# A code-dense step moved behind four products, and two filler matmuls near the start

## The chip, the cores and the metric

The kernel runs on one core of a Trainium2 chip. The metric is the device time in microseconds (us); lower is better. Engines are named as the profile names them: PE multiplies matrices (PEld is its weight load, which runs beside it), DVE, ACT and POOL are the vector, scalar and general engines, and SP issues the DMAs.

## The reference

Two layers follow each other. For each of 8 batches and 8 heads, 576 positions are gathered into 32 memory slots and read back; the result goes through a gated layer with a causal convolution of five taps:

```python
a = softmax(phi)                             # over the 576 positions, for each slot
k_m, v_m = a^T k, a^T v                      # 32 x 64 for each head
attn = softmax(scale * q k_m^T)              # over the 32 slots
x = attn v_m                                 # 576 x 512 for each batch
gate = sigmoid(sum_k conv_w[k] * shift(x, k))
out = (gate * (x @ w_val)) @ w_out
```

## The kernel before

Each matrix step works on one batch b. The products by `w_val` and the gates are made in halves of 288 positions (s), the last product in chunks of 128 output rows (c, 36 in all). The steps that matter here, by name:

- `phi_turn`, `phi_exp`: the softmax weights of the slots. `slots.b` sums keys and values into them (L467): four heads x five chunks x two groups, 40 small matmuls of 32 columns of weights. Batch 0 does this apart for keys (`slots.0.0.1`, `slots.0.1.1`: group 0 and 1) and values (`slots.0.0.0`, `slots.0.1.0`).
- `slots_inv`, `slots_scale`, `slots_turn`, `slots_place` (L474 to L498, L264): divide by the sums (DVE, then ACT or DVE), transpose on PE, and copy to `kvT`.
- `scores.b.s` (L514) multiplies by q; `scores_turn`, `soft_top`, `soft_exp`, `soft_norm`, `soft_turn` are the second softmax on DVE, POOL and ACT. `soft_turn.b.s` writes the rows pT that the following steps read.
- `conv.b.s` (L626, 40 matmuls) makes the gate's input with the taps already in the weights; from batch 2 on `mix.b.s` (L626, 8 matmuls) makes x, and `tap`, `scaled` and `add` apply the taps on DVE, ACT and POOL.
- `value.b.s.t` (L692): six matmuls of 288 columns for one of four column blocks t. Two blocks share two banks of PSUM, which `gated.b.s.y` (L698, DVE) reads together with the gate and gives back. `gated_high` and `gated_low` (L264, L267) split the result into two parts, which `project.c.y` (L727) multiplies by `w_out`.
- `spread_taps` (L388) repeats the convolution's weights; `warm.n` (L280) is a matmul of n x 128 columns of the identity that nobody reads.

All steps stand in one table, `ORDER`, written out by hand. Each engine executes its instructions in the order in which the table issues them; a star swaps the engine of a step. Nothing else orders them but semaphores between writers and readers.

PSUM has 8 banks of 512 floats. `take` gives a step the banks that have been free longest by the order of the table, and `drop` returns them. So a step that is added or moved in the table also changes which banks later steps get, and whose release they wait for.

In the profile, one float32 matmul of the program stands as two instructions of PE and two of PEld; the 40 matmuls of a slots step are x80 there. The split matmuls of L692 and L727 stand as one each.

Of the kernel before, what the change touches and what calls it, by code (L numbers as in the profile page):

```python
# [53 lines left out]
ORDER = """  # L54
warm.4 warm.4 load_top.0.0 load_w.c.0 load_top.0.1 phi_max.0.0 narrow_size.c.0 phi_open.0.0 phi_max.0.1 phi_open.0.1
narrow_round.c.0 phi_turn.0.0 warm.2 narrow_sign.c.0 load_kv.0.0.1 phi_turn.0.1 warm.2 phi_place.0.1 phi_place.0.0*
load_kv.0.1.1 slots.0.0.1 load_w.v.1 narrow_size.v.1 slots.0.1.1 narrow_add.c.0 load_q.0.0 slots_inv.0.1
narrow_round.v.1 spread_taps.1 slots_scale.0.1 place_taps.1 load_w.o.0 load_top.1 slots_turn.0.1 narrow_sign.v.1
narrow_round.o.0 narrow_size.o.0 slots_place.0.1* load_q.0.1 load_kv.0.0.0 scores.0.0 narrow_add.v.1 scores_turn.0.0
soft_top.0.0 phi_max.1 warm.4 soft_exp.0.0 load_kv.0.1.0 phi_open.1.0 warm.4 spread_taps.0 scores.0.1 place_taps.0  # L60
# [20 lines left out]
place.2 add.1.0.1.4 store.0 slots_place.2 phi_shift.3 scores.2.0 load_kv.3.0 tap.1.0.1.3 place.3 scaled.1.0.2.1  # L81
load_rest.3 scaled.1.0.3.1 scores.2.1 value.1.0.0 scaled.1.0.3.2 scores_turn.2.0 add.1.0.1.2 add.1.0.1.1 load_kv.3.1
load_top.4 scores_turn.2.1 value.1.0.1 soft_top.2* open_gate.1.0.0 gated.1.0.0 phi_exp.3 soft_exp.2 add.1.0.1.3
conv.1.1 slots.3 gate.1.1.1 gated_high.1.0.0 soft_norm.2 value.1.1.2 gate.1.1.0 phi_max.4 slots_inv.3 open_gate.1.0.1
value.1.1.3 gated.1.1.1 soft_turn.2.0 slots_scale.3* value.1.0.2 load_q.3 value.1.0.3 gated.1.0.1 gated_low.1.0.0
value.1.1.0 mix.2.0 gated_high.1.1.1 scaled.2.0.2.1 scaled.2.0.2.4 scaled.2.0.3.0 gated_low.1.1.1* value.1.1.1
scaled.2.0.2.0 tap.2.0.1.0 scaled.2.0.3.1 gated_high.1.0.1* slots_turn.3 project.5.0 gated.1.1.0 load_rest.5
project.4.0 soft_turn.2.1 tap.2.0.1.3 tap.2.0.0.0 store.3 scaled.2.0.2.3 slots_place.3* tap.2.0.0.4 gated_low.1.0.1
tap.2.0.1.1 scaled.2.0.3.3 gated_high.1.1.0 scaled.2.0.3.4 load_rest.4 project.4.1 load_top.5 tap.2.0.0.2 load_kv.4.0
# [735 lines left out]
```

## Time and profile before

| | us |
|---|---|
| three runs | 236.61, 237.48, 239.53 (median 237.48) |
| the profiled execution | 237.75 |
| its span, first to last instruction | 236.0 |
| PE busy | 226.2 (96%) |
| DVE / ACT / POOL busy | 185.4 / 169.4 / 170.2 |

The profile describes the execution of 237.75 us; 1.75 us of it lie outside the span. Start times count from the start of the span. A matmul's end is modelled, so a stretch is best measured from the start of its first matmul to the start of the next step's first.

### The profile page before, as it was taken

What the parts mean: (1) busy time and instruction counts of PE and PEld (TensorE: products, weight loads), DVE (VectorE), ACT (ScalarE), POOL (GpSimd) and SP (SyncE); (2) the same over time, 40 slices, a digit from 0 to 9 for tenths busy, and PEclk for the clock granted to TensorE, in tenths of its full rate; (3) what the DMA queues carried; (4) which work ended last, traced back from release to release, by engine and by line L of the source; (5) the groups of instructions that cost most, each with busy time, mean ns of one, the idle gap of its engine ahead of it and who ended that gap; (6) DMA issues with size and microseconds to landing.
All of it is one profiled execution on the core that took longest, in us unless ns stands there. A gap on an engine that the chain in (4) does not pass through costs nothing.

```text
span 236.0 us, 6170 instructions
## 1 busy us (share of the span) xinstructions
PE 226.2 (96%) x2496; PEld 175.1 (74%) x2496; DVE 185.4 (79%) x304; ACT 169.4 (72%) x338; POOL 170.2 (72%) x132
## 2 busy tenths in 40 slices
PE   7788999999989999999999999999999999999994
PEld 2536688777677589677887869787886687888882
DVE  2258828998868999978989879998999979759330
ACT  3369999659738797988878877498898654894302
POOL 1244879979866987999887979589958785955600
PEclk9979999999999999999999999999999999999998
DMA  6999999959958985376741999603801211121114
GB/s 190 372 413 404 416 410 385 416 207 335 364 138 287 420 287 219 99 274 227 247 157 37 327 375 350 259 0 111 267 7 44 87 49 46 44 92 44 44 64 159
DMA packets 14653, 51.17 MB, mean 217 GB/s; under 512 B 1658, under 2 KB 1954, under 8 KB 11938
## 3 DMA queue, kind: packets, MB, share of 16 engines
q1 hardware_dynamic: 14626, 50.79, 58.5%
q8 instruction: 19, 0.31, 0.6%
q14 instruction: 8, 0.07, 0.1%
HBM read 41.35 MB, written 9.44 MB: 215 GB/s over the span
## 4 chain that ended last, share of the span: by engine, by line
PE 90%; DMA 4%; ACT 2%; SPq 1%; issue 1%; POOL 1%
PE banks L727 43%; PE banks L692 22%; PE banks L467 8%; PE banks L626 6%; PE banks L514 4%; DMA q<-in_first_dram 4%; PE banks L593 3%; PE banks L280 1%; PE banks L436 1%; PE banks L498 1%; POOL w_val_sb L381 1%; PE banks L388 1%; ACT o L367 0%; SPq L308 0%; SPq L341 0%
## 5 line engine op out<-in xcount | busy, mean ns | idle before, releaser
L670 POOL TENSOR_TENSOR gate<-gate,x 128x576 f32<-128x576 f32 x49 | 71.7, 1464 | 15.4 <-ACT gate L662 5.3
L727 PE MATMUL banks<-woH,hL 128*128 128x512 f32 x144 | 58.2, 404 | 0.0
L727 PE MATMUL banks<-woH,hH 128*128 128x512 f32 x144 | 56.4, 392 | 0.0
L727 PE MATMUL banks<-woL,hH 128*128 128x512 f32 x144 | 56.3, 391 | 0.0
L662 ACT ACTIVATE x<-banks,cwP 128x288 f32<-128x288 f32 x104 | 48.6, 529 | 5.7 <-PE banks L626 3.7
L653 DVE SCALAR_TENSOR_TENSOR gate<-banks,cwP,gate 128x288 f32<-128x288 f32 x104 | 49.1, 508 | 2.1 <-ACT gate L651 1.2
L267 POOL TENSOR_TENSOR hL<-h,hH 128x576 fp32r<-128x576 f32 (+8 forms) x38 | 38.0, 1019 | 7.8 <-DVE hH L264 4.5
L698 DVE SCALAR_TENSOR_TENSOR h<-gate,banks 128x576 f32<-128x576 f32 x32 | 23.9, 749 | 16.5 <-PE banks L692 12.5
L727 PEld LDWEIGHTS banks<-woH,hL 128*128 128x128 f32 x144 | 27.0, 188 | 9.3 <-issue 2.1
L727 PEld LDWEIGHTS banks<-woH,hH 128*128 128x128 f32 x144 | 27.0, 188 | 6.0
L741 ACT ACTIVATE o<-banks 128x512 f32<-128x512 f32 x26 | 15.7, 603 | 21.1 <-PE banks L727 19.6
L727 PEld LDWEIGHTS banks<-woL,hH 128*128 128x128 f32 x144 | 27.1, 188 | 4.6
L692 PE MATMUL banks<-pL,vwH 128*128 128x288 f32 x128 | 28.6, 305 | 0.0
L692 PE MATMUL banks<-pH,vwH 128*128 128x288 f32 x128 | 27.3, 294 | 0.0
L692 PE MATMUL banks<-pH,vwL 128*128 128x288 f32 x128 | 27.3, 294 | 0.0
L692 PEld LDWEIGHTS banks<-pL,vwH 128*128 128x128 f32 x128 | 21.2, 188 | 6.1 <-issue 3.6
L264 ACT CAST hH<-h 128x576 fp32r<-128x576 f32 (+8 forms) x38 | 18.8, 531 | 7.3 <-DVE h L698 7.3
L267 POOL TENSOR_TENSOR pL<-pT,pH 128x1152 fp32r<-128x1152 f32 (+1 forms) x8 | 19.0, 2372 | 6.4 <-DVE pH L264 6.4
L467 PE MATMUL banks<-kv,e 128*32 128x129 f32 (+2 forms) x656 | 19.3, 263 | 2.8 <-issue 1.4
L675 ACT ACTIVATE gate<-gate 128x576 f32<-128x576 f32 x26 | 18.1, 699 | 4.0 <-DVE gate L653 2.8
L467 PEld LDWEIGHTS banks<-kv,e 128*32 128x32 f32 x656 | 16.3, 128 | 5.7 <-issue 5.3
L692 PEld LDWEIGHTS banks<-pH,vwL 128*128 128x128 f32 x128 | 20.5, 188 | 0.0
(96 smaller groups left out, 369.5 us busy)
## 6 DMA issues: line engine op xcount, KB each, us to landing
kv<-in_kv_dram SPq DMA_DIRECT2D x14, 1032.0 KB, 8.2
out_dram<-o SPq DMA_DIRECT2D x35, 256.0 KB, 2.6
q<-in_q_dram SPq DMA_DIRECT2D x7, 1152.0 KB, 8.4
phT<-in_phi_t_dram SPq DMA_DIRECT2D x7, 576.0 KB, 6.8
e<-in_phi_dram SPq DMA_DIRECT2D x6, 640.0 KB, 7.0
raw<-in_w_val_dram SPq DMA_DIRECT2D x4, 512.0 KB, 10.9
q<-in_first_dram SPq DMA_DIRECT2D x2, 576.0 KB, 9.7
rest<-in_kv_rest_dram SPq DMA_DIRECT2D x4, 258.0 KB, 2.9
```

Of the source, the lines that this page charges most:

```text
L264: eng.copy(out=out, in_=x) if eng is nc.scalar else eng.tensor_copy(out=out, in_=x)
L267: eng.tensor_tensor(out=out, in0=x, in1=hi.bitcast(F32), op=ALU.subtract)
L467: nc.tensor.matmul(km[j * M:(j + 1) * M, i, n], lhsT=e[:, i, j * M:(j + 1) * M, c], rhs=kvx[c][:, j, :], start=(c == 0), stop=(c == C - 1))
L626: nc.tensor.matmul(live["cv", b, s, g][x * D:(x + 1) * D, t, 0:n], lhsT=weights(g)[rows], rhs=pTs[b % 2][rows, g, s * HALF + i:s * HALF + ...
L653: nc.vector.scalar_tensor_tensor(out=gt, in0=v, scalar=w, in1=gt, op0=ALU.mult, op1=ALU.add)
L662: nc.scalar.activation(out=live[n][:, x], in_=live["cv", b, s, g][:, x, i:i + HALF], func=AF.Identity, scale=cwP[:, 0, i * NP + t:i * NP + ...
L670: eng.tensor_tensor(out=gt, in0=gt, in1=live["x", b, s, g, i], op=ALU.add)
L675: nc.scalar.activation(out=gt, in_=gt, func=AF.Tanh, scale=0.5)
L692: nc.tensor.matmul(vp[:, x, 0:HALF], lhsT=a[:, g, t * P:(t + 1) * P], rhs=p[:, g, s * HALF:(s + 1) * HALF], start=(i == 0), stop=(i == len ...
L698: nc.vector.scalar_tensor_tensor(out=h, in0=live["gate", b, s, y], scalar=1.0, in1=live["vp", b, s, y][:, :, 0:HALF], op0=ALU.add, op1=ALU ...
L727: nc.tensor.matmul(live["proj", c][:, 0], lhsT=ring[a][:, t, at:at + P], rhs=w[:, t], start=(y == 0 and i == 0), stop=(y == 1 and i == len ...
L741: nc.scalar.activation(out=o, in_=x, func=AF.Copy, scale=0.5)
```

## The change

Only the table changes. Two `warm.2` (256 columns each) are added: one behind `slots.0.0.1`, one behind `slots.0.1.1`, which are the keys' slots of batch 0. And `slots.3`, `slots_inv.3` and `slots_scale.3` are written later: `slots.3` behind `value.1.0.3` in place of ahead of `value.1.1.2`, `slots_inv.3` behind `gated.1.0.1`, `slots_scale.3` behind `gated_high.1.1.1`. The relative order of all other steps stays. Two of the lines:

```diff
-load_kv.0.1.1 slots.0.0.1 load_w.v.1 narrow_size.v.1 slots.0.1.1 narrow_add.c.0 load_q.0.0 slots_inv.0.1
+load_kv.0.1.1 slots.0.0.1 warm.2 load_w.v.1 narrow_size.v.1 slots.0.1.1 warm.2 narrow_add.c.0 load_q.0.0 slots_inv.0.1
...
-conv.1.1 slots.3 gate.1.1.1 gated_high.1.0.0 soft_norm.2 value.1.1.2 gate.1.1.0 phi_max.4 slots_inv.3 open_gate.1.0.1
+conv.1.1 gate.1.1.1 gated_high.1.0.0 soft_norm.2 value.1.1.2 gate.1.1.0 phi_max.4 open_gate.1.0.1 value.1.1.3
```

PE near the start, the difference of the two programs; kv_77 and kv_78 are the tiles of keys of the two groups, ident the identity of the fillers:

```order
 L280 MATMUL banks<-ident 128x256
 L467 MATMUL banks<-kv_77,e 32x65 x20
+L280 MATMUL banks<-ident 128x256
 L467 MATMUL banks<-kv_78,e 32x65 x16
 L467 MATMUL banks<-kv_77,e 32x65 x4
+L280 MATMUL banks<-ident 128x256
 L388 MATMUL banks<-cw_sb,pick_head 128x64 x5
 L498 MATMUL banks<-ident,kvd 128x128
```

One filler now stands between the two groups of keys, the other ahead of `spread_taps.1` (L388) and `slots_turn.0.1` (L498).

PE around `slots.3` in the kernel before, with the semaphores that each row waits for; L626 is the end of `conv.1.1`, the first L692 is `value.1.1.2`:

```order
L626 MATMUL banks<-pT_75,taps 64x288 x38
L467 MATMUL banks<-kv_77,e 32x129 [waits DMAHW0_49,Activation_49]
L467 MATMUL banks<-kv_77,e 32x129 x15
L467 MATMUL banks<-rest,e 32x129 [waits DMAHW1_49]
L467 MATMUL banks<-rest,e 32x129 x3
L467 MATMUL banks<-kv_78,e 32x129 [waits DMAHW2_49]
L467 MATMUL banks<-kv_78,e 32x129 x15
L467 MATMUL banks<-rest,e 32x129 x4
L692 MATMUL banks<-pL,vwH 128x288 [waits DVE_49]
```

The 40 matmuls of `slots.3` follow directly on the 40 of `conv.1.1`, and the products come after them. PE in the changed kernel, from the end of `conv.1.1` to the third of the four products, `value.1.0.2`:

```order
L626 MATMUL banks<-pT_75,taps 64x288 x38
L692 MATMUL banks<-pL,vwH 128x288 [waits DVE_49]
L692 MATMUL banks<-pL,vwH 128x288
L692 MATMUL banks<-pH,vwL 128x288 x2
L692 MATMUL banks<-pH,vwH 128x288 x2
L692 MATMUL banks<-pL,vwH 128x288 x2
L692 MATMUL banks<-pH,vwL 128x288 x2
L692 MATMUL banks<-pH,vwH 128x288 x2
L692 MATMUL banks<-pL,vwH 128x288 [waits Activation_49]
```

The four products (24 matmuls) now follow on `conv.1.1`, and `slots.3` after them, with `value.1.1.0` behind it as the first product that did not move. The same release of banks by DVE (`gated.1.0.0`) is now waited for right behind `conv.1.1`.

DVE around the same place, the difference; L408 is `phi_max.4`, the rows L698 are `gated.1.1.1` and `gated.1.0.1`, L568 between them is `soft_turn.2.0`, L267 is `gated_low.1.1.1`:

```order
 L408 TENSOR_REDUCE top<-phT 128x2
-L474 TENSOR_SCALAR ri<-banks 128x2
-L475 RECIPROCAL ri<-ri 128x2
-L698 SCALAR_TENSOR_TENSOR h<-gate,banks 128x576
-L568 STREAM_TRANSPOSE pT_73<-st 128x2x288
-L698 SCALAR_TENSOR_TENSOR h<-gate,banks 128x576
+L698 SCALAR_TENSOR_TENSOR h<-gate,banks 128x576
+L568 STREAM_TRANSPOSE pT_73<-st 128x2x288
+L698 SCALAR_TENSOR_TENSOR h<-gate,banks 128x576
+L474 TENSOR_SCALAR ri<-banks 128x2
+L475 RECIPROCAL ri<-ri 128x2
 L267 TENSOR_TENSOR hL<-h,hH 128x2x288
```

`slots_inv.3` (L474, L475) stands behind the two gated products and the transpose now. On ACT `slots_scale.3` passes one step, `gated_high.1.1.1`; POOL and SP keep their order. The banks are dealt anew from the first filler on: the second pair of `mix.2.0` is now the pair that `gated.1.0.1` gives back, and `value.1.1.2` waits for `gated.1.0.0` in both.

## Rows read from the trace of the kernel before

**Rows 1.** The page: busy time by engine, and the packets that bring instructions.

```profile
PE 226.2 (96%) x2496; PEld 175.1 (74%) x2496; DVE 185.4 (79%) x304; ACT 169.4 (72%) x338; POOL 170.2 (72%) x132
...
q8 instruction: 19, 0.31, 0.6%
```

**Rows 2.** Longest of PE's waits over the span: us in total, times, longest.

```profile
PE banks L467 <- issue: 1.4, 1, 1.4
```

**Rows 3.** Timeline of PE, 59.5 to 73: start, us, instructions.

```profile
59.86 2.68 PE L626 MATMUL banks<-pT,taps 32*64 32x288 f32 x80
62.47 1.11 PE L467 MATMUL banks<-kv,e 128*32 128x129 f32 x32
...
63.63 0.83 PE L467 MATMUL banks<-kv,e 128*32 128x129 f32 x21
65.90 0.55 PE L467 MATMUL banks<-kv,e 128*32 128x129 f32 x10 [1.44 <-issue]
...
66.71 0.54 PE L692 MATMUL banks<-pL,vwH 128*128 128x288 f32 x2
...
69.99 0.43 PE L692 MATMUL banks<-pL,vwH 128*128 128x288 f32 x2
...
70.88 0.75 PE L626 MATMUL banks<-pT,kvd 32*64 32x292 f32 x16
```

**Rows 4.** Timeline, 85 to 105: `slots.4` and the step behind it.

```profile
96.28 2.44 PE L467 MATMUL banks<-kv,e 128*32 128x129 f32 x80
...
98.64 0.50 PE L727 MATMUL banks<-woH,hL 128*128 128x512 f32 x1
```

**Rows 5.** Stretches: us, busy (count) PE, PEld, DVE, ACT, POOL; clock, DMA, GB/s.

```profile
59.86:64.46 4.60, 4.60 (x142) 3.39 (x141) 3.99 (x4) 3.44 (x6) 4.10 (x3) 1.00 0.96 390
...
94.05:98.65 4.60, 4.60 (x118) 2.98 (x116) 4.09 (x6) 4.17 (x9) 4.60 (x5) 1.00 0.13 22
```

**Rows 6.** DMA queues in 53.8 to 63.6, and then in 63.6 to 64.65.

```profile
q1 hardware_dynamic: 790, 3.77, 97.2%
...
q8 instruction: 1, 0.02, 6.1%
```

**Rows 7.** Timelines of DVE and POOL, 59 to 75.

```profile
62.06 0.75 DVE L698 SCALAR_TENSOR_TENSOR h<-gate,banks 128x576 f32<-128x576 f32 x1
...
65.31 1.29 DVE L408 TENSOR_REDUCE top<-phT 128x2 f32<-128x1152 f32 x1
...
68.70 0.75 DVE L698 SCALAR_TENSOR_TENSOR h<-gate,banks 128x576 f32<-128x576 f32 x1 [1.53 <-PE banks L692]
69.38 0.77 DVE L568 STREAM_TRANSPOSE pT<-st 128x576 f32<-128x576 f32 x1
...
65.54 2.13 POOL L559 TENSOR_TENSOR st<-st,ss 128x1152 f32<-128x1152 f32 x1 [1.42 <-DVE ss L558]
```

**Rows 8.** Timelines of PE and DVE near the start.

```profile
7.62 0.60 PE L280 MATMUL banks<-ident 128*128 128x256 f32 x2
8.34 0.78 PE L467 MATMUL banks<-kv,e 128*32 128x65 f32 x40
10.37 0.77 PE L467 MATMUL banks<-kv,e 128*32 128x65 f32 x40 [1.25 <-DMA kv<-in_first_dram]
...
12.33 0.33 PE L498 MATMUL banks<-ident,kvd 128*128 128x128 f32 x1
13.29 1.22 PE L514 MATMUL banks<-q,kvT 64*32 64x288 f32 x16 [0.64 <-DMA q<-in_first_dram]
...
18.49 0.72 PE L514 MATMUL banks<-q,kvT 64*32 64x288 f32 x16
...
12.69 0.29 DVE L264 COPY kvT<-banks 128x128 f32<-128x128 f32 x1 [0.81 <-PE banks L498]
```

**Rows 9.** Two stretches near the start, columns as in rows 5.

```profile
9.42:12.83 3.41, 2.29 (x51) 1.96 (x51) 0.76 (x4) 1.10 (x2) 0.00 (x0) 1.00 1.01 374
12.84:16.25 3.41, 2.96 (x18) 1.09 (x19) 1.70 (x4) 2.46 (x5) 1.28 (x1) 0.50 1.04 420
```

More of the change, by code (lines that the diff above doesn't have):

```diff
@@ L83 @@
 load_top.4 scores_turn.2.1 value.1.0.1 soft_top.2* open_gate.1.0.0 gated.1.0.0 phi_exp.3 soft_exp.2 add.1.0.1.3
-conv.1.1 slots.3 gate.1.1.1 gated_high.1.0.0 soft_norm.2 value.1.1.2 gate.1.1.0 phi_max.4 slots_inv.3 open_gate.1.0.1
-value.1.1.3 gated.1.1.1 soft_turn.2.0 slots_scale.3* value.1.0.2 load_q.3 value.1.0.3 gated.1.0.1 gated_low.1.0.0
-value.1.1.0 mix.2.0 gated_high.1.1.1 scaled.2.0.2.1 scaled.2.0.2.4 scaled.2.0.3.0 gated_low.1.1.1* value.1.1.1
+conv.1.1 gate.1.1.1 gated_high.1.0.0 soft_norm.2 value.1.1.2 gate.1.1.0 phi_max.4 open_gate.1.0.1 value.1.1.3
+gated.1.1.1 soft_turn.2.0 value.1.0.2 load_q.3 value.1.0.3 slots.3 gated.1.0.1 slots_inv.3 gated_low.1.0.0 value.1.1.0
+mix.2.0 gated_high.1.1.1 slots_scale.3* scaled.2.0.2.1 scaled.2.0.2.4 scaled.2.0.3.0 gated_low.1.1.1* value.1.1.1
 scaled.2.0.2.0 tap.2.0.1.0 scaled.2.0.3.1 gated_high.1.0.1* slots_turn.3 project.5.0 gated.1.1.0 load_rest.5
```

## The prediction

> **What bounds the kernel now.** Read the shares first: PE is busy 96% of the span and no other engine reaches 80% [rows 1]. So the time is PE's work plus PE's holes, and the next view is the list of PE's own waits. The longest there is put down to no engine and no DMA, but to "issue": 1.4 us at L467 [rows 2]. The other six waits of PE lie near the start, so this is the one hole of the dense part. The timeline then tells where it is. `conv.1.1` runs from 59.86, `slots.3` starts at 62.47, and at 64.46 (63.63 + 0.83) it stops in the middle of the second group's 32 instructions, whose first 21 have run on the same operands; it goes on at 65.90 [rows 3]. A missing operand would hold the first of them, not the 22nd.
>
> What is missing are instructions. The program's matmuls and weight loads are 2 x 2496, and the instruction queue brought 19 packets [rows 1], one for each 263 of them; no other engine issues enough to need as many. In the 4.60 us up to the hole PE and PEld executed 142 + 141 = 283, at a DMA share of 0.96 [rows 5]. From 53.8 to 63.6 no packet of that queue ran, while the data queue held 97% of the DMA engines; one ran between 63.6 and 64.65 [rows 6], and 1.25 us after the end of that stretch PE went on. So two dense steps in a row used up a packet's worth faster than the next came. The second densest place shows the contrast: `mix.3.0` with `slots.4` executed 118 + 116 = 234 in an equal stretch at a DMA share of 0.13 [rows 5], with no hole.
>
> [...]
>
> **The moved slots: the hole.** `slots.3` takes 66.71 - 62.47 = 4.24 us now [rows 3]. The same 80 instructions undisturbed take 98.64 - 96.28 = 2.36 [rows 4]. The hole therefore costs 4.24 - 2.36 = 1.88 us, 1.44 of it as idle time and the rest as the restart. In the changed kernel 24 products (48 instructions) stand between the dense steps. They take 69.99 - 66.71 = 3.28 us [rows 3], where 48 instructions of slots take 48/160 x 2.36 = 0.71. So the same count of instructions lasts 2.57 us longer, and a packet that comes when it does now arrives in time: instruction 283 from the start of `conv.1.1` is then number 75 or so of the 160 of `slots.3`, reached at 62.9 + 3.28 + 75/160 x 2.36 = 67.3, where PE would now be able to go on at 65.9. **Term: -1.88**, between 0 and that.
>
> **The moved slots: a new wait on PE.** `value.1.1.2` waits for `gated.1.0.0` to give its banks back, which DVE ends at 62.06 + 0.75 = 62.81 [rows 7]. Before, slots filled that time; now PE is there at 62.47. With 0.1 us for the signal it starts at 62.9: **+0.43**, and nothing else on PE can pass it. This end of DVE hangs on `scores.2`, which the change doesn't touch. The third product waits for a gate of ACT that is done earlier than PE gets there.
>
> **The moved slots: who waits next.** PE then runs four products (3.28), `slots.3` (2.36) and `value.1.1.0` (70.88 - 69.99 = 0.89): 62.9 + 6.53 = 69.43 is where it reaches `mix.2.0`, which starts at 70.88 now [rows 3]. That step now needs the banks of `gated.1.0.1`. DVE ends `phi_max.4` at 65.31 + 1.29 = 66.60, does `gated.1.1.1` (0.75) without its wait of 1.53, waits for POOL until 65.54 + 2.13 = 67.67, does `soft_turn.2.0` (0.77) and `gated.1.0.1` (0.75): 69.2 [rows 7], 69.3 with the signal. So `mix.2.0` waits for nothing by 0.1 us: **0**, up to +0.5 if DVE or POOL is that much later. `slots_inv.3` and `slots_scale.3` end some 1.5 us later against the table than before, but their reader `slots_turn.3` is a further product away, and its own reader, `scores.3`, some 6 us. SP's queue holds the next load of the `rest` tile until `slots.3` has read it, and this and the loads and stores behind it start some 1.7 us later; what they bring is used no earlier than batches 4 and 5, so that costs nothing. If it did, slots or a `phi_max` of these batches would show a DMA wait.
>
> From `mix.2.0` on all is 1.88 - 0.43 = 1.45 us earlier, and ACT, DVE and POOL, which wait for PE there, with it. Since PE has no hole later, I carry 1.45 to the end.
>
> **The fillers.** The first stands in PE's wait of 1.25 us for the second group's keys; two such instructions take 0.60 [rows 8]: **0**. The second stands ahead of work that waits for no DMA. It pushes L388 and with it `slots_turn.0.1` (12.33) by 0 to 0.60; taking 0.45, and of that the slack ahead of L514, which waits until 13.29 for q (the copy it also needs ends at 12.69 + 0.29 = 12.98), `scores.0.0` starts 0.2 to 0.5 later. Its reader DVE, and behind it POOL, ACT and the first `conv`, follow it, so this is on the path. [...] Net: **-0.1** (-0.3 to +0.1) if it stays, +0.2 to +0.6 if it falls again.
>
> **The sum.** -1.88 + 0.43 + 0 + 0 - 0.1 = -1.55 against the profiled 237.75: 236.2. The median of the runs is 0.27 lower, which gives 235.9; as the runs spread over 2.9 us and the hole of one execution need not be the median's, I round to 236.0.
>
> **The rivals.**
> First, the clock falls all the same: -1.45 + 0.4 = -1.05, so 236.4. For it: fillers of 0.6 us each against holes of 1.25 and 0.64.
> Second, DVE is late at `mix.2.0`: its margin is 0.1 us, and POOL's 2.13 us step ahead of it is rough in the records; at +0.5 the time is 236.5.
> Third, the hole is smaller or missing in the executions that were timed, since it hangs on how full the DMA queues are at 58 to 64 us. Then the new wait of 0.43 stays without its gain: 237.48 + 0.43 - 0.1 = 237.8 at worst, 237.2 if half the hole is there.
> Fourth, on the other side, the hole goes along with `slots.3`. The place is the second half of `slots.3`; the mechanism is that the packet is asked for and served later, or that something in the step itself holds it. PE reaches `mix.2.0` at 62.9 + 3.28 + 4.24 + 0.89 = 71.31 in place of 70.88: +0.43 - 0.1, so 237.8, slower than before. It decides from the packet's end: PE needs it at 67.3 - 1.25 = 66.05, 1.4 us later than it ended here, and slower than before needs another 1.45, so an end after 67.5. Against it speaks that the data queue is nearly empty by then, and that `slots.4` has no hole.
> That the change isn't carried out as written is no case: the order of the instructions shows it.
>
> **How the numbers follow.** The forecast, 236.0, gets 0.56; the clock falling 0.16 (236.4); DVE late 0.07 (236.5); the hole small in the timed runs 0.09 (237.2 to 237.8); the hole moving along 0.12 (237.8). The forecast's own spread is about 0.9 either way, from the terms' bounds (0.5) and from medians of runs that differ by 2.9. The range goes from 234.8, below which lies perhaps one in ten of the first two cases, to 238.0, above which lies some of the last two. The bound of 2% is 4.75 us, about what a measurement of this kernel can tell from no change. No case reaches it; faster by more gets 0.04 for a start that hangs together better than I see, slower by more 0.03 for a wait in the banks dealt anew that I overlooked.
>
> **What would show it.** In the changed kernel's profile: no "issue" entry of a us or more in PE's waits in the dense part; `slots.3` as one row of 80 in about 2.4 us; a start of `value.1.1.2` some 0.4 us after `conv.1.1`'s last matmul, released by DVE; `mix.2.0` about 1.4 us earlier counted from `conv.1.1`; a granted clock of 1.00 from 12.8 to 16.3 and L514 in about 0.72 there. The prediction is wrong if the hole stands again in a later dense step, if PE gets a new DVE wait at L626 near 69, or if the first `conv` starts more than 0.3 us later than before.

## The result and the profile after

| | changed kernel | kernel before |
|---|---|---|
| median of 20 runs each | 239.03 us (237.6 to 242.04) | 237.55 us (236.08 to 240.96) |
| ratio of the two | 1.0053, 95% interval 1.0032 to 1.0074 | |
| profiled execution | 239.06 us, span 237.3 | 237.75 us, span 236.0 |

The change made the kernel slower, by 0.0053 x 237.55 = 1.26 us. That is clear of the noise of 20 runs, and well inside 2%. Forecast were 236.0 and a range that ended at 238.0. The ratios leave out executions more than 1.5% above the fastest of their kernel, so a ratio need not be that of the two medians; of two profiled executions that lie there, e1's (441.59 us) is not used, and no size in the argument rests on e4's (240.3 us).

The page of the changed kernel, its busy line and the granted clock in 40 slices, answers to [rows 1]:

```profile
PE 227.1 (96%) x2500; PEld 175.1 (74%) x2500; DVE 185.5 (78%) x304; ACT 169.6 (71%) x338; POOL 170.1 (72%) x132
...
PEclk9999999999999799999999999999999999999999
```

The shares have hardly moved, and the sums can't tell where 1.3 us went. The clock tells a part of it: slice 14 (77.1 to 83.1 us) has a 7 in place of a 9. The list of PE's own waits answers to [rows 2] (us in total, times, longest):

```profile
PE banks L593 <- ACT o L741: 2.0, 1, 2.0
...
PE banks L692 <- DVE h L698: 0.3, 1, 0.3
```

The entry "issue" of 1.4 us is gone, and so the hole; the wait for DVE at L692 that the forecast priced is there; and at the top stands an entry that the forecast did not have, L593 waiting for ACT. PE's timeline shows all three (start, us, instructions, and idle time ahead with its releaser); the first part answers to [rows 3], the last two rows to [rows 4]:

```profile
58.95 2.68 PE L626 MATMUL banks<-pT,taps 32*64 32x288 f32 x80
61.95 0.53 PE L692 MATMUL banks<-pL,vwH 128*128 128x288 f32 x2 [0.31 <-DVE h L698]
...
65.32 1.12 PE L467 MATMUL banks<-kv,e 128*32 128x129 f32 x32
...
66.47 1.06 PE L467 MATMUL banks<-kv,e 128*32 128x129 f32 x32
...
67.69 0.53 PE L692 MATMUL banks<-pL,vwH 128*128 128x288 f32 x2
...
68.68 0.75 PE L626 MATMUL banks<-pT,kvd 32*64 32x292 f32 x16
...
76.06 1.20 PE L514 MATMUL banks<-q,kvT 64*32 64x288 f32 x32
79.22 1.82 PE L593 MATMUL banks<-w_val_sb,kvT 64*32 64x512 f32 x16 [1.96 <-ACT o L741]
...
97.64 2.44 PE L467 MATMUL banks<-kv,e 128*32 128x129 f32 x80
100.00 0.50 PE L727 MATMUL banks<-woH,hL 128*128 128x512 f32 x1
```

`slots.3` now runs in one piece, 65.32 to 67.69, and `mix.2.0` starts 68.68 - 58.95 = 9.73 us behind `conv.1.1`, where it was 70.88 - 59.86 = 11.02 [rows 3]: 1.29 us won. From `mix.2.0` to the step behind `slots.4` it now takes 100.00 - 68.68 = 31.32 us, where it was 98.64 - 70.88 = 27.76 [rows 3, 4]: 3.56 us lost. All of it lies between 76 and 83. The rows of the kernel before at the same place, from the timelines of SP, PE and ACT:

```profile
66.81 0.33 SPq L317 DMA_DIRECT2D rest<-in_kv_rest_dram  x1
...
70.36 0.44 SPq L747 DMA_DIRECT2D out_dram<-o  x1
...
78.26 1.20 PE L514 MATMUL banks<-q,kvT 64*32 64x288 f32 x32
...
78.67 0.60 ACT L741 ACTIVATE o<-banks 128x512 f32<-128x512 f32 x1
...
79.25 1.15 PE L593 MATMUL banks<-w_val_sb,kvT 64*32 64x512 f32 x16
```

And of the changed kernel, SP's issues and ACT's step:

```profile
57.33 0.34 SPq L324 DMA_DIRECT2D q<-in_q_dram  x1
67.81 0.33 SPq L317 DMA_DIRECT2D rest<-in_kv_rest_dram  x1
68.19 0.42 SPq L747 DMA_DIRECT2D out_dram<-o  x1
68.67 0.42 SPq L317 DMA_DIRECT2D kv<-in_kv_rest_dram  x1
69.20 0.55 SPq L290 DMA_DIRECT2D phT<-in_phi_t_dram  x1
69.79 0.64 SPq L308 DMA_DIRECT2D kv<-in_kv_dram  x1
70.47 0.43 SPq L747 DMA_DIRECT2D out_dram<-o  x1
...
78.57 0.60 ACT L741 ACTIVATE o<-banks 128x512 f32<-128x512 f32 x1 [2.12 <-DMA out_dram<-o]
```

L747 (`store.c`) is the store of one chunk of the output from a buffer `o`, of which there are three. L741 (`place.c`, on ACT) copies the two banks of `project.c` from PSUM into such a buffer. L593 is `val_rows.2`, which takes a bank that `place.5` gives back. SP waits for `slots.3` to have read the `rest` tile, and only then issues, one behind the other, a load of 258 KB, a store, a second load of 258 KB, loads of 576 and 1,032 KB, and last `store.1`. The chain of waits (start, us, what) names the rest of the way:

```profile
70.47 8.01 DMA out_dram<-o
...
78.57 0.61 ACT o L741
...
79.22 1.82 PE banks L593 x16
```

`store.1`, 256 KB, lands 8.01 us after its issue, behind some 2.1 MB of loads. `place.5` waits for its buffer until 78.57, and PE for `place.5`'s bank until 79.22. In the kernel before, the same store took as long from its issue at 70.36 (KB, us to landing):

```profile
out_dram<-o SPq DMA_DIRECT2D x1, 256.0 KB, 8.2
```

There `place.5` started at 78.67, almost the same moment, but PE got to `scores.3.0`, the step ahead of `val_rows.2`, 2.2 us later and found the bank given back just in time. The store is late only against PE. Counted from `conv.1.1`, `place.5` starts 78.57 - 58.95 = 19.62 us behind it in place of 78.67 - 59.86 = 18.81, 0.81 later, while PE comes 1.29 earlier. So most of PE's new wait is the gain of the hole, taken back; the smaller part is the delay of SP. The windows (columns as in [rows 5]; the first answers to the second of [rows 9]) show what came on top:

```profile
12.84:16.25 3.41, 3.35 (x27) 1.65 (x28) 2.50 (x4) 1.79 (x3) 2.17 (x2) 1.00 1.04 421
79.45:82.86 3.41, 3.41 (x34) 0.92 (x19) 1.48 (x2) 1.53 (x3) 3.41 (x3) 0.50 0.99 390
```

Near the start the clock was 1.00 with the fillers, where it had been 0.50. After the wait of 1.96 us it fell to half for 3.41 us in the middle of dense work. The loss of 3.56 splits by rows into two: from `scores.3.0` (L514) to `val_rows.2` 79.22 - 76.06 = 3.16 in place of 79.25 - 78.26 = 0.99, which is 2.17; and from `val_rows.2` to the end of `slots.4` 100.00 - 79.22 = 20.78 in place of 98.64 - 79.25 = 19.39, which is 1.39 and the clock's. Over the whole span: the start up to `conv.1.1` 58.95 in place of 59.86 (-0.91), the two stretches -1.29 and +3.56, what follows 137.3 in place of 137.4 (-0.1): +1.3 together, the difference of the spans.

### The profile page after: what moved, and what is told of

Same layout as the page of the kernel before. It is cut to its first block, busy times and chain, and to the rows that moved or that the text cites. A ratio compares the mean times of both kernels' runs of the same rounds, so it can differ in the third digit from the quotient of the medians.

```text
span 237.3 us, 6180 instructions
## 1 busy us (share of the span) xinstructions
PE 227.1 (96%) x2500; PEld 175.1 (74%) x2500; DVE 185.5 (78%) x304; ACT 169.6 (71%) x338; POOL 170.1 (72%) x132
## 4 chain that ended last, share of the span: by engine, by line
PE 79%; DMA 9%; DVE 4%; ACT 3%; POOL 1%; SPq 1%; issue 1%; DVEq 0%; ACTq 0%; POOLq 0%
PE banks L727 41%; PE banks L692 19%; PE banks L467 6%; PE banks L626 5%; DMA kv<-in_first_dram 4%; PE banks L593 4%; DMA out_dram<-o 3%; PE banks L514 3%; DMA phT<-in_first_dram 1%; POOL st L559 1%; ACT st L547 1%; PE banks L422 1%; PE banks L436 1%; DVE st L521 1%; ACT o L367 1%
## 5 line engine op out<-in xcount | busy, mean ns | idle before, releaser
L267 POOL TENSOR_TENSOR hL<-h,hH 128x576 fp32r<-128x576 f32 (+8 forms) x38 | 38.0, 1016 | 6.2 <-ACT hH L264 3.2
L698 DVE SCALAR_TENSOR_TENSOR h<-gate,banks 128x576 f32<-128x576 f32 x32 | 23.8, 748 | 16.5 <-PE banks L692 12.1
L741 ACT ACTIVATE o<-banks 128x512 f32<-128x512 f32 x26 | 15.7, 604 | 23.6 <-PE banks L727 19.5
L692 PE MATMUL banks<-pL,vwH 128*128 128x288 f32 x128 | 28.7, 305 | 0.3 <-DVE h L698 0.3
L692 PE MATMUL banks<-pH,vwL 128*128 128x288 f32 x128 | 27.3, 294 | 0.0
L692 PE MATMUL banks<-pH,vwH 128*128 128x288 f32 x128 | 27.3, 294 | 0.0
L692 PEld LDWEIGHTS banks<-pL,vwH 128*128 128x128 f32 x128 | 21.2, 188 | 6.9 <-issue 3.8
L267 POOL TENSOR_TENSOR pL<-pT,pH 128x1152 fp32r<-128x1152 f32 (+1 forms) x8 | 18.9, 2360 | 6.4 <-DVE pH L264 6.4
L692 PEld LDWEIGHTS banks<-pH,vwL 128*128 128x128 f32 x128 | 20.4, 188 | 0.0
L692 PEld LDWEIGHTS banks<-pH,vwH 128*128 128x128 f32 x128 | 20.4, 188 | 0.0
```

The lines of the kernel that those rows point to most:

```text
L267: eng.tensor_tensor(out=out, in0=x, in1=hi.bitcast(F32), op=ALU.subtract)
L692: nc.tensor.matmul(vp[:, x, 0:HALF], lhsT=a[:, g, t * P:(t + 1) * P], rhs=p[:, g, s * HALF:(s + 1) * HALF], start=(i == 0), stop=(i == len ...
L698: nc.vector.scalar_tensor_tensor(out=h, in0=live["gate", b, s, y], scalar=1.0, in1=live["vp", b, s, y][:, :, 0:HALF], op0=ALU.add, op1=ALU ...
L741: nc.scalar.activation(out=o, in_=x, func=AF.Copy, scale=0.5)
```

## The experiments

**The theories.** A, the store that is late against PE: the loss is `store.1` in SP's queue behind the wait for `slots.3`, then `place.5`, a bank, and PE; the move by itself is worth what the forecast said, and will show it once the store is early or its buffer isn't needed. B, the fillers: the loss is theirs. C, the move: four products ahead of `slots.3` disturb PE's order as such (banks dealt anew, the wait of 0.3), and the wait at L593 only replaces another. Within A it is open what of the loss is the wait and what is the clock.

No kernel changes the computation; results of filler matmuls are read by nobody in any of them. Every run was timed beside the kernel before on the same chip, so its median stands in each paragraph.

The table has two stretches in PE's timeline of each profiled execution, as above: from `conv.1.1` to `mix.2.0`, from there to the step behind `slots.4`, and their sum. It also has the moment at which `conv.1.1` starts.

| kernel | conv.1.1 at | to mix.2.0 | to behind slots.4 | sum |
|---|---|---|---|---|
| before | 59.86 | 11.02 | 27.76 | 38.78 |
| changed | 58.95 | 9.73 | 31.32 | 41.05 |
| e2 fillers only | 59.41 | 10.07 | 28.69 | 38.76 |
| e3 changed, early stores | 60.14 | 9.72 | 27.76 | 37.48 |
| e4 before, early stores | 61.56 | 11.87 | 27.77 | 39.64 |
| e5 changed, 4 buffers `o` | 60.58 | 9.74 | 27.76 | 37.50 |
| e6 behind two products | 59.60 | 9.74 | 27.77 | 37.51 |
| e7 changed, PE kept busy | 59.67 | 9.73 | 29.66 | 39.39 |
| e8 move only | 60.08 | 9.74 | 29.14 | 38.88 |
| e9 two products, fillers, 4 `o` | 59.31 | 9.73 | 27.77 | 37.50 |
| e10 before, 4 buffers `o` | 59.58 | 11.06 | 27.79 | 38.85 |
| e11 move only, 4 `o` | 60.81 | 9.73 | 27.81 | 37.54 |

Read its last column first: every kernel in which `slots.3` moved and PE does not wait for `store.1` has 37.5, 1.3 below before; every kernel without a move has 38.8 or more; those that have the whole move and PE's wait have 38.9 (e8), 39.4 (e7) and 41.1 (changed).

**The two parts apart.** The move without the fillers:

```diff
-load_kv.0.1.1 slots.0.0.1 warm.2 load_w.v.1 narrow_size.v.1 slots.0.1.1 warm.2 narrow_add.c.0 ...
+load_kv.0.1.1 slots.0.0.1 load_w.v.1 narrow_size.v.1 slots.0.1.1 narrow_add.c.0 ...
```

> Only the move of the fourth batch's slots, without the two fillers. Theory A (the hole in the slots is gone, but the loads and stores on SP's queue now start later against PE's work, a store lands late, and the copy of an output chunk on ACT and the next product of PE wait for it): the time stays above the kernel before, ratio 1.002 to 1.008, no hole inside slots.3, and PE waits 1 to 2 us at the val_rows step of batch 2 for ACT. Rival B (the fillers, or the banks that they deal anew, cost the time): the move alone wins its 1.4 us, ratio 0.993 to 0.996.

Median 239.73 beside 237.54, ratio 1.0058 (1.0027 to 1.0088). For rows, the same kernel ran again:

> Only the move of the slots, once more, for a profile that shows the stretch from 60 to 85 us. Theory A: ratio 1.003 to 1.009, no hole in slots.3, ACT waits 1.5 to 2.5 us for a store at the copy of chunk 5, PE waits 1 to 2 us at val_rows.2.

Median 238.08 beside 237.74, ratio 1.0026 (0.9993 to 1.0059), and ACT's wait 1.45: both a little under what was expected. PE's and ACT's timelines and the window behind:

```profile
79.04 0.60 ACT L741 ACTIVATE o<-banks 128x512 f32<-128x512 f32 x1 [1.45 <-DMA out_dram<-o]
...
79.69 1.09 PE L593 MATMUL banks<-w_val_sb,kvT 64*32 64x512 f32 x16 [1.29 <-ACT o L741]
...
79.00:83.00 4.00, 3.31 (x39) 1.76 (x40) 3.37 (x4) 2.71 (x6) 4.00 (x3) 1.00 1.03 411
```

The new wait is there without fillers, so B falls for it: the move alone gives back all that it wins. In this execution the wait was 1.29 us and the clock stayed at 1.00 behind it.

The fillers without the move:

```diff
-load_kv.0.1.1 slots.0.0.1 load_w.v.1 narrow_size.v.1 slots.0.1.1 narrow_add.c.0 ...
+load_kv.0.1.1 slots.0.0.1 warm.2 load_w.v.1 narrow_size.v.1 slots.0.1.1 warm.2 narrow_add.c.0 ...
```

> Only the two fillers, slots.3 where it was. Theory A: the hole of about 1.4 us inside slots.3 stays, no wait of PE at val_rows.2, ratio 0.997 to 1.002 (the granted clock near 13 us may stay up, worth up to 0.5 us). Rival B: the fillers or the banks carry the loss, ratio 1.003 to 1.008.

Median 236.84 beside 237.54, ratio 0.9971 (0.9938 to 1.0004): not told from no change. PE's and ACT's timelines:

```profile
63.18 0.62 PE L467 MATMUL banks<-kv,e 128*32 128x129 f32 x16
64.48 0.68 PE L467 MATMUL banks<-kv,e 128*32 128x129 f32 x16 [0.68 <-issue]
...
77.86 2.13 PE L593 MATMUL banks<-w_val_sb,kvT 64*32 64x512 f32 x16
...
78.25 0.60 ACT L741 ACTIVATE o<-banks 128x512 f32<-128x512 f32 x1 [0.99 <-DMA out_dram<-o]
```

Two things that were not sought. The hole stands after 32 + 8 + 16 = 56 matmuls of `slots.3`, where it was after 32 + 8 + 21 = 61 [rows 3]. The fillers put four matmuls and their weight loads, 8 instructions, ahead, and the hole came about as many earlier. Counted from the start of the program it stands at the same place: up to the moment at which PE goes on, the windows (columns as in [rows 5]) have 983 matmuls and 983 weight loads in the kernel before and 982 and 983 in e2.

```profile
0.00:65.89 65.89, 59.59 (x983) 42.32 (x983) 45.18 (x75) 48.45 (x90) 42.90 (x41) 0.97 0.91 351
...
0.00:64.47 64.47, 58.54 (x982) 42.10 (x983) 44.24 (x73) 47.98 (x89) 42.48 (x40) 1.00 0.93 358
```

e10 and e4, below, have 983 and 983 too. So the hole goes with the count of instructions, not with an operand. In all four a packet of the instruction queue had begun ahead of PE's going on: in the kernel before at 63.6, 2.3 us ahead of 65.90; in e4 between 65.9 and 66.2, 2.25 to 2.55 ahead of 68.45; in e2 between 62.0 and 63.0, ahead of 64.48; in e10 between 63.3 and 64.3, ahead of 65.66.

The hole was shorter here (0.68), PE was 0.95 us early at `mix.2.0`, and at once the wait for `store.1` showed: `val_rows.2` takes 77.86 to 79.91 in place of about 1.1 us. SP was not late here: it issued `store.1` at 69.14, 9.73 us behind `conv.1.1`, where it was 10.50 before. In the kernel before, `store.1` was about to bind, and PE's coming 0.95 us earlier was enough to find it.

**The store early.** `store.3` and `store.1` go right behind `load_q.3`, ahead of the load of `rest` that waits for `slots.3`:

```diff
-gated.1.1.1 soft_turn.2.0 value.1.0.2 load_q.3 value.1.0.3 slots.3 gated.1.0.1 ...
+gated.1.1.1 soft_turn.2.0 value.1.0.2 load_q.3 store.3 store.1 value.1.0.3 slots.3 gated.1.0.1 ...
...
-... tap.2.0.0.0 store.3 scaled.2.0.2.3 ... load_kv.4.0 store.1 gated_low.1.1.0* ...
+... tap.2.0.0.0 scaled.2.0.2.3 ... load_kv.4.0 gated_low.1.1.0* ...
```

> The changed kernel, with the stores of chunks 3 and 1 issued ahead of the load that waits for slots.3, right behind the load of q for batch 3; the same bytes move. Theory A: the copy of chunk 5 on ACT waits for no store, PE doesn't wait at val_rows.2, the clock stays up there, and the whole gain shows: 1.9 to 3 us under the changed kernel, ratio to the kernel before 0.991 to 0.997. Rival B: as the changed kernel, ratio 1.003 to 1.007. Rival C (the transfers just move and another one ends late): the wait shows at another step of PE within 10 us, ratio 0.999 to 1.005.

Median 236.6 beside 237.54, ratio 0.9968 (0.9942 to 0.9994). Timelines of SP, ACT and PE:

```profile
58.94 0.88 SPq L747 DMA_DIRECT2D out_dram<-o  x2
68.99 0.34 SPq L317 DMA_DIRECT2D rest<-in_kv_rest_dram  x1
...
77.53 0.60 ACT L741 ACTIVATE o<-banks 128x512 f32<-128x512 f32 x1
...
78.23 1.06 PE L593 MATMUL banks<-w_val_sb,kvT 64*32 64x512 f32 x16
```

Both stores go out 10 us ahead of `rest`, ACT and PE wait for nothing at the old place, and the stretch behind `mix.2.0` is 27.76 to the hundredth of before. Nothing else was changed, so C falls. The same edit in the kernel before:

> The kernel before with the two stores issued early in the same way, slots.3 and the hole unchanged. Theory A: the store's landing (78.58 us there) was just in time for the copy at 78.67, so the stores alone win 0 to 0.5 us: ratio 0.997 to 1.001, hole of 1.4 us still there. If the early stores were good by themselves, and not by what slots.3 delays, the ratio would be as low as that of the changed kernel with early stores.

Median 238.15 beside 237.54, ratio 0.9998 (0.9959 to 1.0037). Early stores by themselves show no gain, since there PE still has its hole and comes late enough. The hole is still there, at the same place (2.29 us in this execution):

```profile
65.33 0.83 PE L467 MATMUL banks<-kv,e 128*32 128x129 f32 x21
68.45 0.55 PE L467 MATMUL banks<-kv,e 128*32 128x129 f32 x10 [2.29 <-issue]
```

**The buffer.** The same wait taken away in another place: a fourth `o`, so that `place.5` doesn't need the buffer of `store.1`. SP's order stays.

```diff
-BUFS = {... "gate": 6, "h": 3, "o": 3, "q": 1, ...
+BUFS = {... "gate": 6, "h": 3, "o": 4, "q": 1, ...
```

> The changed kernel with four buffers for output chunks in place of three, so that the copy of chunk 5 no longer needs the buffer that the late store of chunk 1 gives back; SP's order and all transfers stay. Theory A (the late landing reaches PE only through that buffer): no wait of ACT for a store at chunk 5 near 75 to 78 us, no wait of PE at val_rows.2, ratio to the kernel before 0.993 to 0.999, as with the early stores. Rival (the loads behind slots.3 are late in themselves): PE waits elsewhere near there, ratio 1.002 to 1.007.

Median 236.52 beside 237.74, ratio 0.9945 (0.9917 to 0.9972). ACT's and PE's timelines:

```profile
77.99 0.60 ACT L741 ACTIVATE o<-banks 128x512 f32<-128x512 f32 x1
...
78.69 1.06 PE L593 MATMUL banks<-w_val_sb,kvT 64*32 64x512 f32 x16
```

Two independent cuts through the same chain, one at SP and one at the buffer, both give 37.5. With the buffer alone, in the kernel before:

> The kernel before with four buffers for output chunks, nothing else. Theory A: the buffer matters only where slots.3 holds SP's loads against PE; here the hole in slots.3 stays at 0.7 to 2.3 us and PE didn't wait for chunk 5, so ratio 0.997 to 1.001. If the fourth buffer were the gain by itself, 0.993 to 0.996.

Median 237.4 beside 237.45, ratio 1.0005 (0.9978 to 1.0032), with a hole of 1.49 us at the same place. And the move with the buffer but without the fillers:

> The move of the slots with four buffers, without the fillers. Beside the run with fillers (0.9945) it sizes them where nothing else holds the time: theory, from the half clock near 13 us in which the first scores took 0.5 us longer and from a second filler that costs up to 0.45, the fillers are worth 0 to 0.6 us, so ratio 0.994 to 0.998 here. No hole in slots.3 and no wait of PE at val_rows.2.

Median 236.82 beside 237.45, ratio 0.9968 (0.9939 to 0.9997).

**Moving less.** In the kernel before, `slots.3` behind two products only, no fillers, so that SP's wait for it ends earlier:

```diff
-conv.1.1 slots.3 gate.1.1.1 ... phi_max.4 slots_inv.3 open_gate.1.0.1
-value.1.1.3 gated.1.1.1 soft_turn.2.0 slots_scale.3* value.1.0.2 ...
+conv.1.1 gate.1.1.1 ... phi_max.4 open_gate.1.0.1 value.1.1.3 slots.3
+gated.1.1.1 slots_inv.3 slots_scale.3* soft_turn.2.0 value.1.0.2 ...
```

> The kernel before with slots.3 behind two products of the four, no fillers. Theory A: 24 instructions between the two dense steps last 1.3 us longer than those of slots that they displace, so the hole of 1.4 to 1.9 us shrinks to about half a us; SP's loads start half as late against PE's work, so PE's wait at val_rows.2 is 0 to 0.6 us and the clock holds: ratio 0.995 to 1.001. If every step of the move cost in proportion, the ratio would be 1.002 to 1.004.

Median 236.52 beside 237.74, ratio 0.9954 (0.9925 to 0.9982). PE's timeline has no hole at all, and ACT's lists no wait:

```profile
64.39 1.11 PE L467 MATMUL banks<-kv,e 128*32 128x129 f32 x32
...
65.54 1.06 PE L467 MATMUL banks<-kv,e 128*32 128x129 f32 x32
...
77.20 0.60 ACT L741 ACTIVATE o<-banks 128x512 f32<-128x512 f32 x1
```

Half the distance is enough against the hole. With 12 matmuls of products ahead, PE's 983rd from the start is the ninth of the row at 65.54, so PE gets to it at about 65.8 (an estimate, at 1.06 us for the row's 32), 6.2 us behind `conv.1.1`; in the kernel before and in e10 PE went on 6.04 and 6.08 us behind it, no later than that. The shorter move also keeps SP early enough, but barely: `store.1` is issued 10.27 us behind `conv.1.1` and lands 7.2 us later, and `place.5` starts 17.60 us behind `conv.1.1`, 0.2 later than in e3 (17.39) and e5 (17.41). With the fillers and the fourth buffer on top:

> The version that the runs point to: slots.3 behind two products, both fillers, four buffers for output chunks. Theory A: no hole in slots.3, no store in the way of chunk 5, clock up near 13 us: ratio 0.991 to 0.996, at or under the two best so far (0.9945, 0.9954). If the gains don't add, since each only uncovers the same slack, 0.994 to 0.998.

Median 236.69 beside 237.45, ratio 0.9963 (0.9936 to 0.9991). No gain over e5 or e6; the intervals of e3, e5, e6, e9 and e11 all overlap, so no one of them is shown to be best. All five beat both kernels.

**The clock's share.** The changed kernel with two matmuls of 512 columns on `ident` ahead of `val_rows.2`, in a free bank, so that PE works during its wait. The helper issues them `times` times and puts the order of the banks back, so that no other step gets another bank:

```diff
-tap.2.0.0.3 scores.3.1 val_rows.2 scores_turn.3.0 ...
+tap.2.0.0.3 scores.3.1 warm.4.2 val_rows.2 scores_turn.3.0 ...
```

> The changed kernel with two matmuls of 512 columns of the identity, which nobody reads, right ahead of val_rows.2, in a bank that is free there; they leave all other steps their banks. They take 0.9 to 1.8 us of PE, inside its wait. Theory A, its part on the clock (the wait of 2 us lets the clock fall for some 3.4 us, which costs 1.2 us more): the wait for the store stays, the clock holds at full, and 0.5 to 1.3 us of the loss come back: ratio 1.000 to 1.004. If the clock is no part of the loss: ratio 1.005 to 1.010.

Median 238.55 beside 237.74, ratio 1.0042 (1.0017 to 1.0066). PE's and ACT's timelines:

```profile
76.78 1.20 PE L514 MATMUL banks<-q,kvT 64*32 64x288 f32 x32
77.91 1.98 PE L280 MATMUL banks<-ident 128*128 128x512 f32 x4
79.83 1.09 PE L593 MATMUL banks<-w_val_sb,kvT 64*32 64x512 f32 x16
...
79.10 0.60 ACT L741 ACTIVATE o<-banks 128x512 f32<-128x512 f32 x1 [1.93 <-DMA out_dram<-o]
```

ACT's wait is nearly as long as in the changed kernel (1.93 and 2.12), and `val_rows.2` starts 79.83 - 76.78 = 3.05 us behind `scores.3.0`, against 3.16; but from there to the end of `slots.4` it is 19.23 us and not 20.78. In the profiled execution the two parts of the loss are thus told apart: 2.1 us wait, 1.5 us clock. By the medians of the timed runs they are not: 1.0042, just above the 1.000 to 1.004 expected, and 1.0053 lie in each other's interval.

The mean granted clock of every timed run is on record, and it says more. Of the twelve profiled executions used here, seven have a mean of 0.993 or less, each with one stretch of 3.4 us at half somewhere; five have 0.997 or more, without one in the first 230 us. Of the changed kernel's 20 runs 9 stand at 0.993 or less, with a median of 239.9 us, and 11 at 0.997 or more, with 238.67. So in more than half of its runs the clock had no such fall, and these still lie 1.1 us above the median of the kernel before: the wait makes the kernel slower without the clock. In e7 10 of 12 runs stand at 0.997 or more, with a median of 238.44.

## Why the prediction was wrong

**What held.** The hole: `slots.3` took 2.37 us where 2.36 was forecast, and no "issue" entry is left. The new wait of PE: `value.1.1.2` starts 61.95 - 58.95 = 3.00 us behind `conv.1.1` where it was 2.61 [rows 3], +0.39 for +0.43, released by DVE. DVE's instruction ends at 61.14 + 0.75 = 61.89, so the signal took 0.06 us where the sum had 0.1. `mix.2.0` waits for nothing. The longest entry in the list of PE's waits was in fact one of 1.5 us at the program's start; the "issue" of 1.4 is the longest of the dense part, which is what the argument needed. The four products and `value.1.1.0` took 0.19 us more together than the rows that priced them, so that PE was 1.29 early at `mix.2.0` and not 1.45. The fillers: L514 in 0.72 at a clock of 1.00.

**The step that failed** is the end of "who waits next": "this and the loads and stores behind it start some 1.7 us later; what they bring is used no earlier than batches 4 and 5, so that costs nothing". The delay was right (`rest` is issued 67.81 - 58.95 = 8.86 us behind `conv.1.1` in place of 6.95, so 1.9; 1.0 of it is left at `store.1`), and so is what is said of the loads. But a store brings nothing; it gives something back. The question "who reads what this DMA brings?" has an answer for loads only. For `store.1` it should have been "who writes this buffer next?": `place.5`, on ACT, whose bank PE wants for `val_rows.2`. With it falls the sentence "Since PE has no hole later, I carry 1.45 to the end". PE had no hole at `val_rows.2` before only because its other hole had made it late: in the row of before `place.5` starts at 78.67 and `val_rows.2` at 79.25, at about the earliest moment that it could. This second sentence weighs more: had SP's delay cost nothing, `place.5` would still have started 18.81 us behind `conv.1.1`, and PE, 1.29 us early, would have waited there for about as long. The delay adds 0.81. A fall of the clock behind a new wait had no term at all.

For the profiled execution the sum then reads: -1.29 to `mix.2.0`, +2.17 for the wait at `val_rows.2`, +1.39 for the clock behind it. That the store is the cause is shown by e3 and e5, which remove it in two ways and bring back the stretch's 27.76, and by e2, where the same wait shows as soon as PE comes 0.95 us earlier without any move. That the clock has its part is shown for the profiled executions (e7); in the timed runs at most 9 of 20 can have it, and the clock stayed up in e8 after a shorter wait.

**The size of the forecast gain** was too large also where the store doesn't bind. It said -1.55. The stretches give -1.24 to -1.30; the timed runs -0.0055 x 237.74 = -1.31 in e5 (interval -1.97 to -0.67), -1.09 in e6, -0.88 in e9 and -0.76 in e3 and e11.

**The rivals.** The clock near 13 us did not fall, DVE was not late at `mix.2.0`, the hole did not move along with `slots.3`. The third, a smaller hole in the timed runs than in the profile, may hold in part: among runs at a clock of 0.997 or more the medians of e3, e5, e6, e9 and e11 lie 0.6 to 0.95 us under that of the kernel before beside them, where the stretches say 1.3. Its own sum is off: with half the hole, 0.94, it is 237.48 + 0.43 - 0.1 - 0.94 = 236.9 and not 237.2. The fourth rival's time, 237.8 (the third's at worst too), was the nearest to the result, but by a mechanism that is not there. On what holds PE there the runs decide: the hole goes with the count of instructions (56 matmuls in e2, 61 in e4, e10 and before, and the same 983 from the start in all four), it went away with slower steps ahead, and where it stood PE was idle for 0.68 us (e2), 1.44 (before) and 1.49 (e10). So the hole belongs to a place in PE's instructions and not to `slots.3`, which has none in the changed kernel, e3, e5 and e6.

**The fillers** were put at -0.1, a term that no run shows. With them `conv.1.1` starts at 58.95 to 60.58 (six executions, mean 59.7), without them at 59.58 to 60.81 (five, e4's long one left out, mean 60.0), and no pair of timed runs that differs by them alone tells them from nothing. The clock does: the 16 instructions of L514 near 13 us took 0.72 at 1.00 in the changed kernel, where they took 1.22 at 0.50 before [rows 8, 9]. In the six profiled executions with them it was at full near 13 us each time, and one (e5) had a stretch at half later, from 19.7. In the six without them it fell near 13 in three (before, e6, e8) and from 18.5 to 19.3 in two (e11, e4); it stayed up in e10 alone. Of the timed runs of e2, e3, e5, e7 and e9, with fillers, 46 of 59 stand at 0.997 or more; without them, 23 of 46 in e4, e6, e10 and e11, and 47 of 99 of the kernel before. As the runs of the kernel before at the higher clock have medians 0.7 to 1.1 us under the others', an estimate of the fillers' worth is 0.3 x 0.9, some 0.3 us, less what they cost elsewhere. That the clock would stay up with them, as the -0.1 takes it, was right more often than not.

None of the signs that were to show the prediction wrong was the right one; "slots or a `phi_max` of these batches would show a DMA wait" looked at readers of loads again.

## What to carry to other kernels

When a step moves, follow each queue that waits for it to the end of what is queued there, and ask of a store who writes its buffer next, and what that step holds meanwhile: here it was a PSUM bank, two engines away. Before carrying a gain to the end of the kernel, look for the later places where the bottleneck engine arrives just as something is released; they have no wait to be seen in the profile, and take back the gain. When such a chain has been found, cut it where it is cheapest (one more buffer, an earlier store, a shorter move), and only together with the change that needs it: alone, neither the buffer nor the early store showed a gain (1.0005 and 0.9998).

## What the hardware showed that was not expected

- A store of 256 KB took 8.01 us from issue to landing with some 2.1 MB of loads issued in the 2.7 us ahead of it on the same queue; the page's median for the 35 stores is 2.8 us. In the kernel before it took 8.2, and no wait for it is listed there.
- The clock of TensorE was granted at half for 3.41 us after one wait of 1.96 us in dense work, which cost 1.39 us more, and stayed at full after one of 1.29 us in the same place (e8). Near the start it fell in five of six profiled executions without the fillers and in one of six with them; the same table of steps can do either (9 of 20 timed runs of the changed kernel at 0.993 or less). What decides in a single run is not settled here.
- The hole in the issue of PE was 0.68 (e2), 1.44 (before) and 1.49 us (e10), with 2.29 in e4's untypical execution. It stands at the same instruction of the program each time and ends 2.3 us after a packet of the instruction queue has begun in the kernel before, 2.25 to 2.55 us in e4. That its length hangs on when that packet comes and how soon PE gets there is an estimate from these two. It had gone in e6, where only two products stand ahead of `slots.3`.
